# Attention with its order written out per pair of steps, a table of PSUM banks, two more turned heads, and turned rows kept by quarters

## The chip, the cores and the metric

The kernel runs on one core of a Trainium2 chip. A core has five engines, each with its own queue of instructions that it takes in order: TensorE (PE in the profile; PEld is its loading of weights), VectorE (DVE), ScalarE (ACT), GpSimd (POOL) and SyncE (SP, which here only issues transfers). TensorE writes its products into banks of PSUM, from where VectorE and ScalarE read them. Transfers between DRAM and the core's memory run on 16 DMA engines. The metric is the device time of one execution in microseconds; the number given is the median of the runs.

## What is computed

A token mixer of two parallel branches on the same normalised rows: attention with 16 query heads that share one key head and one value head, and a two-layer network with GELU.

```python
S, D, H, Dh, F = 2048, 448, 16, 28, 1792
xn = layernorm(x)
# attention, on layernorm's output
q = (xn @ wq).reshape(S, H, Dh)
k, v = xn @ wk, xn @ wv
p = softmax(einsum("hqd,kd->hqk", q, k) * Dh ** -0.5)
a = einsum("hqk,kd->hqd", p, v) @ wo
# network, with a second normalisation
y = layernorm(xn)
m = gelu(y @ w1 + b1) @ w2 + b2
out = x + a + m
```

All of it is in float32; the kernel keeps most operands as a high and a low part to reach that precision.

## The kernel before

The kernel has three stages. The first loads x, normalises it, turns it and projects it to q, k and v; the projections are also written to DRAM. The second is the network. The third is attention, which runs as 16 units: a unit is one chunk of 512 queries with one group of four heads. A unit has 16 key tiles of 128 keys, taken two at a time, so that attention has 128 steps; two steps in a row are a pair of steps, 64 in all.

**Ordinary heads.** The softmax needs the largest score of each row ahead of time. For each head a stream of 16 products with the queries on the partitions (`max_stream`, L598) is reduced by VectorE (L599). The negated maximum of a unit goes into two extra rows of its queries (`load_max`). In attention each key tile and head then has one product with the keys on the partitions (L1032), and ScalarE takes its exponential into a buffer `p` (L1033). When all four heads of a key tile are there, `pv` multiplies the values with them in four matmuls side by side (L996), summed over the 16 tiles in one bank `po`.

**Turned heads.** For one head of each unit, and two heads of unit 15 (`TURNED`), the product is made once, with the queries on the partitions (`turned_scores`, L632). VectorE copies it into a buffer `raw` and takes its maximum in the same instruction (L633); ScalarE takes the exponential in two halves of 1024 columns (`turned_exp`, L650); four stores write the tile to DRAM (`td`, L653). Later `load_quarters` brings a quarter of the keys back with one transfer for each half of it (L840), and VectorE turns 32 x 32 blocks into the layout that L996 reads (`turn_blocks`, L1008). A turned head thus has 16 products where an ordinary one has 32.

Both streams begin in the second stage, where they fill gaps between the network's matmuls: 390 of the 752 maxima and 192 of the 272 turned products are made before attention. There are two `raw` buffers, so tile t + 2 waits until tile t is stored.

**What sets the order.** Attention's program is written by a loop that reads a string of letters for each pair of steps: s is a score with its exponential, m a maximum, t a turned product, x half an exponential of a turned tile, T a turn, n and o steps of the normalisation and of the output product, e `load_max`, a bar the second step's start, and a figure that many weighted sums. There are six such strings, one for most units' first pairs, one for their others, and four for the start and the end. Letters with nothing to do are passed over; m is held back by a share of the total (`WEIGHTS`, `LEAD`), and a figure takes only tiles of steps that are complete.

**PSUM banks.** Seven banks take scores, maxima, turned products and output products in attention (`m0` to `m6`), and one holds `po`. `mtile` takes the bank that a small plan with fixed prices of each operation believes free first.

Of the kernel before, what the change touches and what calls it, by code (L numbers as in the profile page):

```python
# [10 lines left out]
F32 = mybir.dt.float32  # L11
# [6 lines left out]
P = 128  # L18
S, D, H, DH, F = 2048, 448, 16, 28, 1792
NT = S // P  # L20
CT = 4
# [13 lines left out]
LEAD = 11  # L35
KEPT = 1, 2, 3
MLP_ORDER = 1, 2, 3, 0
NH = 8
# [4 lines left out]
def block_kernel(ctx, tc, x, wq, wk, wv, wo, w1, b1, w2, b2, out):  # L43
# [10 lines left out]
    free_at, clock = {}, dict(pe=0, a=0, d=0)  # L54
# [37 lines left out]
    wqp = ph1a.enter_context(tc.tile_pool(name="wqp", bufs=1))  # L92
    xin, first_raws = [], []
    for c in range(2):
        first_raw = keep.tile([P, 4, NT, 32], F32, name="raw", bufs=RAWS)
        first_raw = first_raw.rearrange("p r b i -> p (r b i)")[:, 0:CT * D].rearrange("p (k d) -> p k d", k=CT)
# [17 lines left out]
        for t in range(t0, t0 + n):  # L114
            nc.sync.dma_start(xin[t], xv[:, t, :])

    def mtile(shape, by="d"):
        if free_at:
            i = min(free_at, key=lambda i: free_at[i])
            clock["pe"] = max(clock["pe"], free_at[i]) + PRODUCT  # L120
            clock[by] = max(clock[by], clock["pe"] + LANDS) + READS[by]
            free_at[i] = clock[by] + LANDS
        else:
            i = banks["d"].popleft()
            banks["d"].append(i)
        return (mp if i < 3 else mp4).tile(shape, F32, name=f"m{i}")

    def rawtile(shape):
# [496 lines left out]

    def turned_scores(i):
        for t in range(CT):
            raw = keep.tile([P, 4, NT, 32], F32, name="raw", bufs=RAWS)
            m3 = keep.tile([P, 8], F32, name="m3", bufs=RAWS)
            for n in range(4):  # L630
                sc = mtile([P, CW])
                pe.matmul(sc, q3[i % 2][:, t * P:(t + 1) * P], ks[:, n * CW:(n + 1) * CW], start=True, stop=True)  # L632
                dve.tensor_scalar(raw[:, :, 4 * n:4 * n + 4, :].rearrange("p r b i -> p b r i"),  # L633
                                  sc.rearrange("p (b r i) -> p b r i", r=4, i=32), SCALE, -3e38,
                                  op0=ALU.mult, op1=ALU.max, accum_out=m3[:, n:n + 1])
# [9 lines left out]
    def turned_exp():  # L645
        if not exps:
            return
        u, t, raw, m3, h = exps.pop(0)
        rs = slice(2 * h, 2 * h + 2)
        act.activation(raw[:, rs], raw[:, rs], AF.Exp, bias=m3[:, 4:5], scale=1.0)  # L650
        if h == 1:
            for a in (0, 2, 1, 3):
                nc.sync.dma_start(td[u].rearrange("(r p) a k -> p a r k", p=32)[:, 4 * t + a],  # L653
                                  raw[32 * a:32 * a + 32].rearrange("p r b i -> p r (b i)"))
            stored[u] = t

    tq = Stream()
# [107 lines left out]
    for n in range(len(mslots) + 2):  # L765
# [22 lines left out]
        if c == NCH - 1 and 6 <= ft < 12:  # L788
            for i in (2 * ft - 12, 2 * ft - 11):
                q, r = divmod(i, 4)  # L790
                nc.sync.dma_start(ahead[q][:, 4 * r:4 * r + 4, :], td[0, 3][:, 4 * r:4 * r + 4, P * q:P * q + P])
        ts, pace = 0, 21
        if n == 2:
            pace = 20
# [25 lines left out]
    free_at.update((i, k) for k, i in enumerate((0, 1, 6, 3, 2, 4, 5)))  # L820

    def weights_tile():
        t = xl_p.tile([P, 4, CW], F32R, name="xl").rearrange("p b n -> p (b n)")
# [17 lines left out]

    pool.memset(wor, 0.0)
    woh = wol = None
# [12 lines left out]
    rows, worked = {}, []  # L856

    def load_rows_of(c, tiles):
        for k in tiles:
# [4 lines left out]
    def o_jobs(c, gs, tiles=range(CT)):  # L864
        last = NG - 1 in gs
        for k in tiles:
            po = mtile([P, D])
            ts = slice(k * P, (k + 1) * P)
            for g in gs:
                oth, otl = ots[c, g]  # L870
                pe.matmul(po, oth[:, ts], woh[:, g, :], start=(g == gs[0]), stop=False)  # L871
                pe.matmul(po, oth[:, ts], wol[:, g, :], start=False, stop=False)  # L872
                pe.matmul(po, otl[:, ts], woh[:, g, :], start=False, stop=(g == gs[-1]))  # L873
            a = rows[c, k]
            dve.tensor_add(a, a, po)
            if last:
                nc.sync.dma_start(ov[:, CT * c + k, :], a)
            worked.append(1)
            yield

    def o_tiles(c, g):
# [141 lines left out]
    def score(u, kt, j):  # L1023
        if not halfway:
            p = pair_of()
            halfway.append((p[:, 1], (id(p), 1)))
            p, key = p[:, 0], (id(p), 0)
        else:
            p, key = halfway.pop()
        taken[key] = u, kt  # L1030
        s = mtile([P, CW], "a")
        pe.matmul(s, ks[:, kt * P:(kt + 1) * P], qss[u][:, j, :], start=True, stop=True)  # L1032
        act.activation(p, s, AF.Exp, scale=SCALE)  # L1033
        ps[u, kt, j] = p
# [13 lines left out]
    left = total - maxed  # L1048
    weight = [0 if n >= len(steps) - LEAD else WEIGHTS[n % 2] for n, (u, kt) in enumerate(steps)]

    def begin(n):
        nonlocal loads
        u, kt = steps[n]
        if n == 0:
            loads = pool
        if n == len(steps) - 6:
            free_at.pop(6)
# [11 lines left out]
    for n0 in range(0, len(steps), 2):  # L1069
# [9 lines left out]
        kind = 0 if n0 == 0 else 5 if n0 >= len(steps) - 2 else 4 if u == NU - 1 else 3 if n0 > len(steps) - LEAD else 1 + (kt0 > 0)  # L1079
        for what in ORDERS[kind]:  # L1080
            if what == "|":
                n, kt = n0 + 1, kt0 + 2
                begin(n)
            elif what == "s":
                score(*jobs.pop(0))
            elif what == "m":
                if maxed < total - left + left * sum(weight[:n + 1]) / sum(weight):
                    maxed += mxs.step()
            elif what == "t":
                if tq.step():  # L1090
                    clock["d"] += 125
            elif what == "x":
                if exps:
                    clock["a"] = max(clock["a"], clock["pe"]) + 1041
                turned_exp()
            elif what == "T":
                if turn:
                    clock["d"] = max(clock["d"], clock["pe"]) + 1165
                    turn_blocks(u, *turn.pop(0))
            elif what == "e":  # L1100
                if kt >= 6 and u + 1 in mrs:
# [1 line left out]
            elif what == "n":  # L1103
                side.step()
            elif what == "o":
                if n >= len(steps) - 5 and not lasts:
                    lasts.append(oside.add(o_jobs(NCH - 1, range(NG - 1))))
                worked.clear()
                oside.step()
                if worked:  # L1110
                    clock["pe"] += 2200
                    clock["d"] += 2000
            elif what.isdigit():
                clock["pe"] += 320
                for _ in range(int(what)):
                    if pvq[0] in steps[:n] or (pvq[0][0], pvq[0][1] - 1) in steps[:n]:
                        pv(*pvq.pop(0))
                        clock["pe"] += 858
# [31 lines left out]
```

## Time and profile before

| | us |
|---|---|
| median of 3 runs (1064.3 to 1064.78) | 1064.61 |
| the profiled execution | 1064.65 |
| its span, first to last instruction | 1062.8 |
| TensorE busy | 1054.0 (99%) |
| VectorE busy | 903.6 (85%) |
| ScalarE busy | 723.5 (68%) |
| GpSimd busy | 563.2 (53%) |
| first score product of attention begins at | 480.8 |

The profile is of one execution. An engine's busy time is the time covered by records of its instructions; on TensorE records of neighbouring matmuls overlap, since the next one begins while the one before is still running out. A group of instructions has its line, engine and operation, what it writes and reads, its count, its busy time and the mean of one record in ns, and the idle time just ahead of its instructions with what ended it. A row of a stage gives its start and end, its length, then the busy time of each engine with the number of instructions, the granted share of TensorE's clock, the mean share of the DMA engines that was busy, and GB/s. A row of the timeline has the start, the length, the engine and the instruction, where instructions of one kind that follow each other are one row.

### The profile page before, as it was taken

The numbers are of one execution on the slowest core, as the hardware profiler recorded it, in microseconds if no ns is written. First come the engines' busy times: TensorE is split into PE (matmuls) and PEld (weight loads), VectorE is DVE, ScalarE is ACT, GpSimd is POOL, SyncE is SP. The second block draws the span as 40 slices with busy tenths as digits, with TensorE's granted clock in tenths as the row PEclk, the third lists the DMA queues.
The fourth block names the chain that finished last, engine by engine and source line by source line (L and its number), as shares of the span: only waits on it lengthen the run. The fifth ranks groups of instructions, "written<-read, shape, count | busy, mean of one in ns | idle before, by whom it ended". The sixth has DMA issues, their size and how long they took to land.

```text
span 1062.8 us, 17825 instructions
## 1 busy us (share of the span) xinstructions
PE 1054.0 (99%) x5805; PEld 711.2 (67%) x5805; DVE 903.6 (85%) x1890; ACT 723.5 (68%) x1240; POOL 563.2 (53%) x704
## 2 busy tenths in 40 slices
PE   9999999999999999999999999999999999999998
PEld 8778888888888888885555455655545644556455
DVE  7889999999999899998888888688887777776765
ACT  6775555655656655646888888588887687775773
POOL 6678787668766778874354434324333334343130
PEclk9999999999999999999999999999999999999999
DMA  9864455566665666955877888778788676775692
GB/s 269 250 225 151 121 152 163 151 187 182 196 182 167 180 205 195 286 165 151 225 230 217 227 235 234 193 222 225 212 235 233 187 215 177 182 182 144 181 286 77
DMA packets 222160, 209.86 MB, mean 197 GB/s; under 512 B 17854, under 2 KB 173668, under 8 KB 222068
## 3 DMA queue, kind: packets, MB, share of 16 engines
q1 hardware_dynamic: 209524, 187.28, 61.5%
q0 software_dynamic: 11136, 20.87, 8.0%
q8 instruction: 46, 0.75, 0.3%
q10 hardware_dynamic: 1408, 0.57, 0.2%
q14 instruction: 46, 0.38, 0.1%
HBM read 121.31 MB, written 86.10 MB: 195 GB/s over the span
## 4 chain that ended last, share of the span: by engine, by line
PE 96%; DVE 3%; ACT 1%; DMA 0%; issue 0%; ACTq 0%; DVEq 0%
PE po L996 20%; PE m L1032 18%; PE m L598 16%; PE m L715 12%; PE ph L192 11%; PE m L632 6%; PE qp L192 3%; DVE mx L599 1%; PE ph L195 1%; PE ph L197 1%; PE m L871 1%; PE m L873 1%; PE m L872 1%; PE po L979 1%; PE m L979 1%; PE qp L316 0%
## 5 line engine op out<-in xcount | busy, mean ns | idle before, releaser
L599 DVE TENSOR_REDUCE mx<-m 128x1 f32<-128x512 f32 x752 | 484.4, 682 | 89.5 <-PE m L598 87.6
L1033 ACT ACTIVATE p<-m 128x512 f32<-128x512 f32 x652 | 342.1, 622 | 102.7 <-PE m L1032 99.8
L598 PE MATMUL m<-ks,qm 128*128 128x512 f32 x752 | 288.5, 399 | 1.0 <-DVE mx L599 0.6
L1032 PE MATMUL m<-xh,ks 128*128 128x512 f32 x752 | 259.6, 413 | 0.5 <-DVE a L720 0.5
L996 PE MATMUL po<-p,vs 128*32 128x512 f32 x1664 | 219.5, 595 | 0.9 <-DVE p L1008 0.9
L1032 PEld LDWEIGHTS m<-xh,ks 128*128 128x128 f32 x752 | 137.6, 187 | 96.5 <-issue 40.0
L633 DVE TENSOR_SCALAR_CACHE_REDUCE raw<-m 128x512 f32<-128x512 f32 x272 | 181.7, 686 | 9.0 <-PE m L632 6.1
L598 PEld LDWEIGHTS m<-ks,qm 128*128 128x128 f32 x752 | 141.3, 188 | 40.8 <-issue 11.7
L650 ACT ACTIVATE raw<-raw,m 128x1024 f32<-128x1024 f32 x136 | 152.9, 1161 | 0.0
L1008 DVE STREAM_TRANSPOSE p<-quarter 128x1024 f32<-128x1024 f32 x114 | 139.9, 1233 | 1.8 <-DMA quarter<-td 1.5
L680 ACT ACTIVATE hx<-ph,b1t 128x512 f32<-128x512 f32 x55 | 37.9, 688 | 150.5 <-PE ph L197 99.0
L996 PEld LDWEIGHTS po<-p,vs 128*32 128x32 f32 x1664 | 55.0, 109 | 108.7 <-issue 105.2
L632 PE MATMUL m<-ks,q 128*128 128x512 f32 x272 | 107.1, 395 | 0.0
L696 POOL TENSOR_TENSOR hl<-hx,hh 128x512 fp32r<-128x512 f32 x56 | 72.7, 1299 | 32.5 <-ACT hh L694 32.4
L563 POOL DMA_DIRECT2D xh<-qd x60 | 37.7, 630 | 86.6 <-PE m L1032 76.7
L715 PE MATMUL m<-w2h,hl 128*128 128x448 f32 x224 | 81.3, 367 | 0.0
L715 PE MATMUL m<-w2h,hh 128*128 128x448 f32 x224 | 81.3, 366 | 0.0
L715 PE MATMUL m<-w2l,hh 128*128 128x448 f32 x224 | 81.2, 366 | 0.0
L684 POOL TENSOR_TENSOR hz<-hz,hx 128x512 f32<-128x512 f32 x56 | 72.8, 1300 | 4.6
L689 POOL TENSOR_TENSOR hx<-hx,hz 128x512 f32<-128x512 f32 x56 | 72.6, 1297 | 4.7
L1033 ACT ACTIVATE xh<-m 128x512 f32<-128x512 f32 x100 | 55.8, 623 | 21.8 <-PE m L1032 21.3
L682 POOL TENSOR_SCALAR hz<-hz 128x512 f32<-128x512 f32 x56 | 35.0, 624 | 56.6 <-ACT hz L681 56.5
(198 smaller groups left out, 1548.8 us busy)
## 6 DMA issues: line engine op xcount, KB each, us to landing
td<-raw SPq DMA_DIRECT2D x272, 256.0 KB
quarter<-td SPq DMA_DIRECT2D x130, 512.0 KB
xh<-qd POOLq DMA_DIRECT2D x56, 168.0 KB, 5.2
qd<-qe SPq DMA_DIRECT2D x24, 256.0 KB
a<-in_A_x_dram SPq DMA_DIRECT2D x24, 224.0 KB
qm<-qd SPq DMA_DIRECT2D x96, 56.0 KB
qm<-qd POOLq DMA_DIRECT2D x92, 56.0 KB, 4.2
ad<-a SPq DMA_DIRECT2D x16, 224.0 KB
```

What stands on the lines that cost most here:

```text
L192: pe.matmul(ps, w, v, start=(n == 0), stop=False)
L598: pe.matmul(pm, qm[:, t * P:(t + 1) * P], ks[:, n * CW:(n + 1) * CW], start=True, stop=True)
L599: dve.tensor_reduce(mx[:, CT * j + t, n:n + 1], pm, axis=AX.X, op=ALU.max)
L632: pe.matmul(sc, q3[i % 2][:, t * P:(t + 1) * P], ks[:, n * CW:(n + 1) * CW], start=True, stop=True)
L633: dve.tensor_scalar(raw[:, :, 4 * n:4 * n + 4, :].rearrange("p r b i -> p b r i"), sc.rearrange("p (b r i) -> p b r i", r=4, i=32), SCALE, ...
L650: act.activation(raw[:, rs], raw[:, rs], AF.Exp, bias=m3[:, 4:5], scale=1.0)
L684: pool.tensor_mul(hz, hz, hx)
L715: pe.matmul(m2[k], h[:, k * P:(k + 1) * P], w[:, ft, :], start=(ft == 0 and i == 0), stop=(ft == NF - 1 and i == 2))
L996: pe.matmul(po[32 * j:32 * j + 32, :], vs[:, kt, :], ps.pop((u, kt, j)), start=(kt == 0), stop=(kt == NT - 1))
L1008: dve.transpose(p.rearrange("p k (g j) -> p g k j", j=32), part[:, :, 32 * k:32 * k + 64].rearrange("p g (k j) -> p g k j", j=32))
L1032: pe.matmul(s, ks[:, kt * P:(kt + 1) * P], qss[u][:, j, :], start=True, stop=True)
L1033: act.activation(p, s, AF.Exp, scale=SCALE)
```

## The change

Three things change together.

1. The six strings become 64, one for each pair of steps, and the plan behind `mtile` becomes a table of 1193 figures, the bank of each tile of attention in turn. The gates on m are gone. A figure may take a key tile as soon as its four heads have been issued, and many strings hold two or three figures.
2. `TURNED` gains the second head of units 11 and 13: 19 turned heads instead of 17.
3. The turned rows lie in DRAM by quarters of the keys. A tile's buffer `raw` is ordered the same way, each product filling one quarter. A store has 32 x 16 runs of 128 elements where it had 32 x 4 of 512; a load of half a quarter has 128 runs of 1024 elements where it had 128 x 8 of 128.

`turned_scores` also passes a step by while more than two halves await their exponential.

```diff
-WEIGHTS = 3, 5
-ORDERS = ("nsmsmsmsonsmsmst|sxnmsmsetssnmTmT2", "nxmnnsso|snsT4mtnsemnmsssmmsosstmsT", "snmTsmsmxnsmn4|smensmmssntsmssotsoT", "sTsnesnx4s|nssssossstsnoT", "TsTTnen4sT|nsssssosno", "nTss4sTonTss|nosTsns2")
-PRODUCT, LANDS, READS = 229, 200, {"a": 480, "d": 602}
-TURNED = tuple((u, 3) for u in range(16)) + ((15, 2),)
+ORDERS = (
+    "|sssmsmssmtmssmmmTssTtss",
+    "sm|ssss3smsttsmsstTssT",
...
+    "Tsss2msnsnstsmmm|sTssssmxxn3",
...
+)
+BANKS = (
+    "0163240513642015346203412503125064312560314526045231604521306451230465123460531246053214062153046123"
...
+)
+TURNED = tuple((u, j) for u in range(16) for j in ((3, 2) if u in (11, 13, 15) else (3,)))
...
-    td = {h: dram.tile([P, 4 * CT, 512], F32, name=f"td{h[0]}_{h[1]}") for h in TURNED}
+    td = {h: dram.tile([4, P, 4 * CT, P], F32, name=f"td{h[0]}_{h[1]}") for h in TURNED}
...
-    def mtile(shape, by="d"):
-        if free_at:
-            i = min(free_at, key=lambda i: free_at[i])
-            clock["pe"] = max(clock["pe"], free_at[i]) + PRODUCT
-            clock[by] = max(clock[by], clock["pe"] + LANDS) + READS[by]
-            free_at[i] = clock[by] + LANDS
-        else:
-            i = banks["d"].popleft()
-            banks["d"].append(i)
+    def mtile(shape):
+        i = int(places.pop(0)) if places else banks["d"][0]
+        banks["d"].append(banks["d"].popleft())
...
-            raw = keep.tile([P, 4, NT, 32], F32, name="raw", bufs=RAWS)
+            while len(exps) > 2:
+                yield
+            raw = keep.tile([P, 4, 4, P], F32, name="raw", bufs=RAWS)
...
-                dve.tensor_scalar(raw[:, :, 4 * n:4 * n + 4, :].rearrange("p r b i -> p b r i"),
+                dve.tensor_scalar(raw[:, n].rearrange("p r (b i) -> p b r i", i=32),
...
-                nc.sync.dma_start(td[u].rearrange("(r p) a k -> p a r k", p=32)[:, 4 * t + a],
-                                  raw[32 * a:32 * a + 32].rearrange("p r b i -> p r (b i)"))
+                nc.sync.dma_start(td[u].rearrange("q (r p) a k -> p a (q r) k", p=32)[:, 4 * t + a],
+                                  raw[32 * a:32 * a + 32].rearrange("p q r k -> p (q r) k"))
...
-            nc.sync.dma_start(part, td[u, j][:, at, P * q:P * q + P])
+            nc.sync.dma_start(part, td[u, j][q, :, at])
...
-        for what in ORDERS[kind]:
+        for what in ORDERS[n0 // 2]:
...
-                if maxed < total - left + left * sum(weight[:n + 1]) / sum(weight):
-                    maxed += mxs.step()
+                maxed += mxs.step()
...
-                    if pvq[0] in steps[:n] or (pvq[0][0], pvq[0][1] - 1) in steps[:n]:
+                    if all((*pvq[0], j) in ps for j in range(4)):
                         pv(*pvq.pop(0))
```

Lines of the changed kernel have other numbers; the instructions that the text speaks of stand there at L668 and L669 (maxima, before L598 and L599), L704 and L705 (turned products, L632 and L633), L1068 (weighted sums, L996), L1080 (turns, L1008), L1104 (scores, L1032), L912 (a mark that a quarter's buffer is free, L839), L725 (stores, L653) and L913 (loads of quarters, L840).

The order of TensorE in the second pair of steps of unit 6, before: scores (`m<-xh,ks`), maxima (`m<-ks,qm`) and one block of sums (`po<-p,vs`, four matmuls for each sum).

```order
L598 MATMUL m_8106<-ks,qm_160 128x512
L1032 MATMUL m_8109<-xh,ks 128x512
L1032 MATMUL m_8117<-xh,ks 128x512
L996 MATMUL po<-p,vs 32x512 x16
L1032 MATMUL m_8140<-xh,ks 128x512
L598 MATMUL m_8143<-ks,qm_160 128x512
L578 MATMUL m_8146<-ident,mr 12x128
L1032 MATMUL m_8155<-xh,ks 128x512
```

The same place now, from the first of its two blocks of sums; the second, of 12 matmuls, stands after 15 products.

```order
L1104 MATMUL m_8107<-xh,ks 128x512
L1068 MATMUL po<-p,vs 32x512 x8
L668 MATMUL m_8119<-ks,qm_163 128x512
L1104 MATMUL m_8122<-xh,ks 128x512
L1104 MATMUL m_8126<-xh,ks 128x512
L1104 MATMUL m_8129<-xh,ks 128x512
L704 MATMUL m_8134<-ks,q_165 128x512
L1104 MATMUL m_8137<-xh,ks 128x512
```

One block of four sums became blocks of two and of three, with products between them; over attention 61 blocks of whole sums become 73.

The order of VectorE in unit 13, before: turns (`p<-quarter`), maxima, and marks of a free quarter.

```order
L1008 STREAM_TRANSPOSE p<-quarter 128x16x2x32
L839 MEMSET quarter 1x1
L599 TENSOR_REDUCE mx<-m_10912 128x1
L1008 STREAM_TRANSPOSE p<-quarter 128x16x2x32
L599 TENSOR_REDUCE mx<-m_10919 128x1
L599 TENSOR_REDUCE mx<-m_10925 128x1
```

And now, in the same unit, where two heads are turned:

```order
L1080 STREAM_TRANSPOSE xh<-quarter 128x16x2x32
L1080 STREAM_TRANSPOSE p<-quarter 128x16x2x32
L912 MEMSET quarter 1x1
L669 TENSOR_REDUCE mx<-m_10947 128x1
L912 MEMSET quarter 1x1
L654 SCALAR_TENSOR_TENSOR mn<-m_10955,mn 12x128
L948 TENSOR_TENSOR a<-a,m_10962 128x448
L1080 STREAM_TRANSPOSE p<-quarter 128x16x2x32 x2
```

Unit 13 has 16 turns where it had 8, in twos at some places. Before the first score of attention, the order of instructions on every engine is the old one but for the shape of the stores and of the first quarters' loads.

More of the change, by code (lines that the diff above doesn't have):

```diff
@@ L28 @@
 PAIRS = 13
-WEIGHTS = 3, 5
-ORDERS = ("nsmsmsmsonsmsmst|sxnmsmsetssnmTmT2", "nxmnnsso|snsT4mtnsemnmsssmmsosstmsT", "snmTsmsmxnsmn4|smensmmssntsmssotsoT", "sTsnesnx4s|nssssossstsnoT", "TsTTnen4sT|nsssssosno", "nTss4sTonTss|nosTsns2")
-PRODUCT, LANDS, READS = 229, 200, {"a": 480, "d": 602}
-TURNED = tuple((u, 3) for u in range(16)) + ((15, 2),)
+ORDERS = (
+    "|sssmsmssmtmssmmmTssTtss",
+    "sm|ssss3smsttsmsstTssT",
+    "smmss|sm3essmtsTxmsssstsT",
+    "T|x4mmsstTssmsssssm2smss",
+    "mmsssmTxxsstmTmss4smn|sntsss",
+    "smm2nmsmsmmsststst|Tntxsmss3enmTsmnxs",
+    "ssssm3TsmnsmssttmsTsss|n",
+    "ssxnmsTtsnxn22msnsmmmssssnsTs|",
+    "ssstT2smsst|msmssssTs",
+    "ssT|2msntmsTstsxmmnsmmx4smsnnstmsts",
+    "|ssmTnmnnTsses3smssstssmsmxmm",
+    "sns3sssTsmm|smnnstmmtm2snssmmsntT",
+    "sssTssxnssm4mnsnmmsss|mtsT",
+    "sss|2mmsmssxtmnnTsmssnxs3snsT",
+    "|tmsmsssstsnssTTe21tmssssx",
+    "sT|smsss1nn4Tmmxsntnssmmsmsss",
+    "sssTmsnnms3Tmsmsmtnsssms|sto",
+    "ntsT4xxsnsnTms|stmnstsmmssmnsnsns",
+    "o2nooTmsmosmosesnsmttmTsm3msmssmsmsno|mnxos",
+    "smTssTmx|4stsmnstsmsstsss",
+    "Ts|mmssT3tsmmmsmsmxmtsossmsnmsnmtsmm",
+    "sns|sTsssnx6nmssmsmTmtsossm",
+    "smsnssmssmmstosmst|sexxTTnss",
+    "ssTmsn213|snsmsmtnsnsTosmmssntns",
+    "sstTsmxstxsts31mstssmTtnss|s",
+    "Tsss2msnsnstsmmm|sTssssmxxn3",
+    "tennmTTstnsssnmssnss4sms|sms",
+    "mssmsssn|tssmTmsTsn3nttssmms",
+    "ssxxmmTnsmssst1T3mntsm|ssnsss",
+    "Ttsnsxtn21s|mnsssxTsmmses2msmss",
+    "ssmtssmsnsstnT|s4xTmsmssms",
+    "nssnstsxmTsm2mTsssssnsmtt|2s",
+    "Tssnmnmtsnstsxxtmmss3on|mmosstnnsTsms",
+    "smT|osso4smesnsmsmmmsssnmsnTs",
+    "smnst2x2T|tsmsnsmssmosmxmosTssns",
+    "msn3|sTmsmnsmossmnsnttsmsstxsTxmos",
+    "sTs5mstsmsstsTmmmsso|tssttmsx",
+    "sTtsoxssststnmnms2xsmmssxnsmnT|s",
+    "ssmsnns5smnesTstmssm|osmssT",
+    "sstsnss|Tmsnn3smtssmmnTsss",
+    "ms|stnxsTm4Tsmssnssssss",
+    "mm|xT2mtnmssnsm11mnnstssmsstsssTs",
+    "sTm2|esnnsmssmtssmnnxmsmxsntT3msstmms",
+    "so|tTstssmmTmm1n3smnssmsssnmmnsms",
+    "|sTsTm5nTmnmnsmsnntssTss",
+    "Ts|ssTTTss5msesnmsm",
+    "ssssxssT111s|TTTs",
+    "snmsssss|nTxsTT5Tntsn",
+    "smmsmsssmsnttsssnnTm|mxsm3mmmnosTs",
+    "Tmsmms|smsn4nmtxesnmstsnTsssmomsts",
+    "nmn3|osmsmsmsmosmnmsossTmTssomsmsn",
+    "4on1TnnmssmnTtsssssm|1smsmssms",
+    "sTm3oTmmssnTnsmnm|omssssT",
+    "msmxnsnomTssTtt4nstnmm|TssnTs",
+    "ssm|sneonTnTssmsmm4TmssT",
+    "mTmsmnsns5xmsTTTs|mmsss",
+    "stsT4mmxnsss|snnossnmssTss",
+    "sxnssmm31ssmTsssssm2Tmsnm|s",
+    "ssmsmTs1enssnssss|snTs",
+    "ss4ssssssTsnns|2Tss",
+    "TnssssssTssT1n|11T",
+    "nnTsss|ssTTsT3ss",
+    "ssssssTn5n|sToTTs",
+    "sTssosTs|sossoT212T",
+)
@@ L94, in block_kernel @@
     for c in range(2):
-        first_raw = keep.tile([P, 4, NT, 32], F32, name="raw", bufs=RAWS)
-        first_raw = first_raw.rearrange("p r b i -> p (r b i)")[:, 0:CT * D].rearrange("p (k d) -> p k d", k=CT)
+        first_raw = keep.tile([P, 4, 4, P], F32, name="raw", bufs=RAWS)
+        first_raw = first_raw.rearrange("p q r k -> p (q r k)")[:, 0:CT * D].rearrange("p (k d) -> p k d", k=CT)
         first_raws.append(first_raw)
@@ L819, in block_kernel @@
     op = ctx.enter_context(tc.tile_pool(name="op", bufs=1, space=PSUM))
-    free_at.update((i, k) for k, i in enumerate((0, 1, 6, 3, 2, 4, 5)))
+    places.extend(BANKS)
+    banks["d"] = collections.deque((0, 1, 2, 3, 4, 5))
     def weights_tile():
@@ L854, in prep_wo @@
         pool.tensor_sub(wol[:, g, :], wor[:, g, :], f(woh[:, g, :]))
-    rows, worked = {}, []
+    rows = {}
     def load_rows_of(c, tiles):
@@ L1047, in block_kernel @@
     total = 4 * CT * len(heads)
-    left = total - maxed
-    weight = [0 if n >= len(steps) - LEAD else WEIGHTS[n % 2] for n, (u, kt) in enumerate(steps)]
     def begin(n):
```

34 lines of the change are left out of this document (15 added, 19 removed).

## The prediction

> **What bounds the kernel now.** I read the first two parts of the page, then the busy time by stage, then the groups of the last stage, then the timeline of TensorE alone. The page:
>
> ```profile
> span 1062.8 us, 17825 instructions
> PE 1054.0 (99%) x5805; PEld 711.2 (67%) x5805; DVE 903.6 (85%) x1890; ACT 723.5 (68%) x1240; POOL 563.2 (53%) x704
> PEclk9999999999999999999999999999999999999999
> PE 96%; DVE 3%; ACT 1%; DMA 0%; issue 0%; ACTq 0%; DVEq 0%
> ```
>
> TensorE is never long idle, its clock is granted in full, and it holds 96% of the chain that ended last. But matmul records overlap, so 99% busy does not say that nothing is lost. By stage (us; TensorE, weight loads, VectorE, ScalarE and GpSimd busy; clock, DMA share, GB/s):
>
> ```profile
> 60.00:430.00 370.00, 368.95 (x1673) 310.57 (x1672) 353.28 (x772) 218.13 (x304) 279.32 (x273) 1.00 0.60 175
> 480.80:1058.70 577.90, 576.49 (x3577) 309.04 (x3575) 454.77 (x896) 437.97 (x827) 204.09 (x323) 1.00 0.75 204
> ```
>
> The second row is attention, from the first score (L1032) to the last matmul: 577.9 us, and all of the reordering is there. Its groups:
>
> ```profile
> L599 DVE TENSOR_REDUCE mx<-m 128x1 f32<-128x512 f32 x362 | 233.5, 676 | 86.2 <-PE m L598 86.2
> L1032 PE MATMUL m<-xh,ks 128*128 128x512 f32 x752 | 259.6, 413 | 0.5 <-DVE a L720 0.5
> L996 PE MATMUL po<-p,vs 128*32 128x512 f32 x1664 | 219.5, 595 | 0.9 <-DVE p L1008 0.9
> L598 PE MATMUL m<-ks,qm 128*128 128x512 f32 x362 | 134.6, 404 | 0.0
> L996 PE MATMUL po<-xh,vs 128*32 128x512 f32 x256 | 64.7, 595 | 0.0
> L632 PE MATMUL m<-ks,q 128*128 128x512 f32 x80 | 31.8, 398 | 0.0
> ```
>
> What one costs is the distance between starts, not the mean of a record. The timeline of TensorE:
>
> ```profile
> 639.22 0.65 PE L1032 MATMUL m<-xh,ks 128*128 128x512 f32 x2
> 639.80 2.35 PE L996 MATMUL po<-p,vs 128*32 128x512 f32 x19
> 641.56 0.59 PE L996 MATMUL po<-xh,vs 128*32 128x512 f32 x1
> ...
> 641.99 0.59 PE L996 MATMUL po<-xh,vs 128*32 128x512 f32 x1
> ...
> 643.37 0.50 PE L1032 MATMUL m<-xh,ks 128*128 128x512 f32 x1
> 643.71 0.39 PE L598 MATMUL m<-ks,qm 128*128 128x512 f32 x1
> 643.94 0.39 PE L1032 MATMUL m<-xh,ks 128*128 128x512 f32 x1
> 644.17 0.62 PE L598 MATMUL m<-ks,qm 128*128 128x512 f32 x2
> ```
>
> From 643.71 to 643.94 and to 644.17, a product of 512 columns takes 0.23 us (0.228 over longer pieces). A weighted sum (four heads, one key tile) is two passes of four matmuls, 0.43 apart (641.56, 641.99): 0.86 us. A block of four sums should take 3.44 and takes 3.57 (639.80 to 643.37); the product ahead of it lasts 0.12 longer than 0.23 and the first one behind it 0.11 longer (0.34). So each change from products to sums and back costs about **0.35 us**, whatever the block's size.
>
> Attention adds up so: 752 + 362 + 80 = 1194 products at 0.228 = 272.2; 240 sums in whole (1920 records by 8) and 16 in halves, 256 at 0.86 = 220.2; 180 output matmuls at 0.20 = 36.0; 65 blocks of sums at 0.35 = 22.8. That is 551.2 of 577.9. Of the other 26.7, some 4 lie behind the last sum and 3 in the small transposes ahead of new maxima. About **20 us** are waits of a product for its PSUM bank, as the waits of the weight loads show (total, times, longest):
>
> ```profile
> PEld m L1032 <- ACT p L1033: 29.9, 136, 0.3
> PEld m L598 <- ACT p L1033: 6.8, 26, 0.3
> ```
>
> Many waits, none over 0.3 us, partly hidden behind the running matmul. VectorE and ScalarE are not full, but they must be fed while TensorE is in its sums, and seven banks are all the stock they have.
>
> **The change part by part.** *Two more turned heads.* Each gives up 16 maximum products and 16 score products for 16 turned ones. The order has 720, 330 and 112 products in attention: 32 fewer, 32 x 0.228 = **-7.3 us** of TensorE. VectorE loses 32 maxima and gains 32 turned reads, 8 small reductions and 16 turns. Its prices, by distance of starts:
>
> ```profile
> 604.16 1.24 DVE L1008 STREAM_TRANSPOSE p<-quarter 128x1024 f32<-128x1024 f32 x1
> 605.33 0.69 DVE L599 TENSOR_REDUCE mx<-m 128x1 f32<-128x512 f32 x1
> ...
> 609.25 1.89 DVE L599 TENSOR_REDUCE mx<-m 128x1 f32<-128x512 f32 x3 [0.67 <-PE m L598]
> 611.06 0.68 DVE L633 TENSOR_SCALAR_CACHE_REDUCE raw<-m 128x512 f32<-128x512 f32 x1
> ```
>
> A turn takes 1.17, a maximum (611.06 - 609.25) / 3 = 0.60, and I take 0.61 for a turned read. So +32 x 0.01 + 8 x 0.08 + 16 x 1.17 = +20 us: from 362 x 0.60 + 80 x 0.61 + 136 x 1.17 + some 20 of small work = 445 to 465 us. That lies beside TensorE while its stage lasts longer. ScalarE gives up 32 exponentials and gains 16 of double width, which is about even. The 32 further stores and 16 further loads go to SP's queue, which does nothing but transfers; I cost them at nothing beside 545 us of TensorE work, until a turn waits for its quarter. On GpSimd the two heads' columns are loaded into the turned heads' buffers instead of the maxima's, 8 loads either way, and its other steps move with the order. What TensorE could wait for there is the next head's columns:
>
> ```profile
> qm<-qd POOLq DMA_DIRECT2D x92, 56.0 KB, 4.2
> ```
>
> They land in 4.2 us. Between their issue and their first use the order has at least 9.5 us of TensorE work before and 11.3 now, so I cost this at nothing too; 16 times some 2 us if GpSimd were held up.
>
> *The order.* The blocks of sums become 76 (73 in whole, 3 in halves), 11 more: 11 x 0.35 = **+3.9 us**. In return the run of products between blocks falls from about 20 to about 16, so fewer products stand behind seven banks. No row shows the new waits. From below they are bounded by nothing (-20 us). From above, two units of this profile, 0 and 1:
>
> ```profile
> 480.80:515.20 34.40, 32.99 (x182) 17.06 (x180) 29.17 (x57) 25.66 (x50) 9.12 (x15) 1.00 0.65 185
> 515.20:550.50 35.30, 35.30 (x211) 17.92 (x211) 30.15 (x63) 31.01 (x60) 18.75 (x27) 1.00 0.78 218
> ```
>
> Unit 1 has 81 products (18.5), 16 sums (13.8) and 4 blocks (1.4): 33.7, so it loses 1.6. Unit 0 has 82, 12 and 3, 30.1, and loses 4.3: its sums start late, and TensorE runs ahead of its readers. So a unit loses 1.6 where the feeding goes well and 4.3 where it does not. Counted in the two orders, products that take a bank last used five or six products before, with no sum between, fall from 196 to 136. By that count 20 us become 14; with shorter blocks, over which the readers' stock lasts better, I take **12**, nearer to the count than to nothing: **-8 us**.
>
> *The bank table* costs no time of its own: it names the bank that the planner chose before, and its worth is in those waits.
>
> *Turned rows by quarters.* A store of 256 KB becomes 512 packets of 512 bytes instead of 128 of 2 KB, a load of 512 KB 128 packets of 4 KB instead of 1024 of 512 bytes; per head 9216 packets instead of 10240. The trace has a stage with many 2 KB stores (60 to 430: 175 GB/s at a share of 0.60, 292 at a full share) and one where 512-byte loads rule (204 at 0.75, 272 at a full share). The four stores of a tile, 1 MB, take 3.6 us of all engines by the first and 3.9 by the second. Is there room? The stage before attention, SP's and VectorE's rows:
>
> ```profile
> 218.51 10.01 SPq L653 DMA_DIRECT2D td<-raw  x8
> 222.46 4.62 DVE L599 TENSOR_REDUCE mx<-m 128x1 f32<-128x512 f32 x7
> 227.38 0.69 DVE L633 TENSOR_SCALAR_CACHE_REDUCE raw<-m 128x512 f32<-128x512 f32 x1 [0.30 <-PE m L632]
> ```
>
> The stores start at 218.51, and the same buffer is written again at 227.38: 8.9 us for 3.9, and VectorE waited there for TensorE, not for a transfer. I cost it at nothing, bounded by 46 tiles before attention at 0.3 either way, 14 us if that cover were gone. Order and counts before attention stay as they are, so its 480.8 us stay.
>
> [...]
>
> **The sum.** The profiled execution took 1064.65 us, 1062.8 of span and 1.85 around it; the runs shown have a median of 1064.61, the same. 1064.65 - 7.3 + 3.9 - 8 = **1053 us**.
>
> **The rivals.**
>
> *All bank waits go.* For it: no wait is over 0.3 us, and both readers have idle time in sum (VectorE 445 of 578). Against: 136 tight reuses remain. It gives 1064.65 - 7.3 + 3.9 - 20 = 1041 us.
>
> *The order moves the waits only.* Eleven more blocks are paid for, and the waits of 20 us stay. For it: bank and reader prices are the same. It gives 1064.65 - 7.3 + 3.9 = 1061 us; with 3 us more of waits it is no change.
>
> *VectorE becomes the limit (slower).* By the order, units 12 and 13 together have 56 maxima, 9 turned reads and 24 turns: 33.6 + 5.5 + 28.1 and some 3.5 of small work = 70.7 us of VectorE. TensorE has 145 products (33.1), 31 sums (26.7), 36 output matmuls (7.2), 9 blocks (3.2): 70.2. No slack is left there, and units 2, 4 and 8 (36 maxima and turned reads each) are near: 21.7 + 9.4 + 0.8 = 31.9 beside some 34 of TensorE. If in each of these five units the loss is unit 0's 4.3 instead of 1.6, and the waits elsewhere stay, 1061 + 13.5 = 1075 us. It decides from 4 us of such losses on, where 1065 is reached. Against it: over all of attention VectorE has 465 of some 565 us, and its reads are spread over the unit.
>
> *The stores are slower than the loads show (slower).* If a 512-byte packet into DRAM took over twice its share, 1 MB would need over the 8.9 us there are, and VectorE would stand still at each of 46 tiles; 1 us each is +46, some 1099 us.
>
> *The change does not do what it says.* The order shows 32 products fewer and 76 blocks, so only the timing is open.
>
> **How the numbers follow.** Chances: the forecast, 1047 to 1059, 0.60; nearly all waits gone, 1041 to 1047, 0.10; waits moved, 1059 to 1067, 0.18; VectorE the limit 0.09; stores 0.03. The range of 1044 to 1067 leaves out half of the second and the last two cases, 0.17. A measurement of this kernel can tell about 0.2% (2.1 us) from no change. Faster by more than that (under 1062.5) are the first two and 0.10 of the third: 0.80; within it 0.08; slower 0.12.
>
> **What would show it.** Attention should end some 12 us earlier with 480.8 us before it unchanged. In its groups L1032 has 720, L598 330 and L632 112. The waits of weight loads for L1033 should fall in sum. Right for the stores: VectorE's turned reads still wait for TensorE and for no DMA. Wrong: waits of TensorE's products for VectorE's maxima or turns in units 12 and 13 (the VectorE rival), sums that wait for a turn, or a longer stage before attention (the stores).

## The result and the profile after

The changed kernel takes **1056.0 us** (median of 4 runs, 1053.39 to 1056.62) where the kernel before takes 1064.65 (1064.3 to 1064.78): a ratio of 0.9915, with a 95% interval of 0.9897 to 0.9932. That is faster by 8.6 us, where 11.6 were forecast; 1056.0 lies in the range. The runs spread over 3.2 us where those of before spread over 0.5.

The page of the changed kernel, profiled in the run of 1055.69 us: span, engines, and the chain that ended last by engine.

```profile
span 1052.8 us, 17905 instructions
PE 1043.8 (99%) x5773; PEld 708.9 (67%) x5773; DVE 926.9 (88%) x1962; ACT 720.6 (68%) x1224; POOL 563.1 (53%) x704
PE 94%; DVE 3%; DMA 1%; ACT 1%; SPq 0%; issue 0%; ACTq 0%; DVEq 0%
```

TensorE still bounds it, VectorE has 23 us more work, and transfers have come into the chain with 1%. The span is 10.0 us shorter, and 1.0 us more lies around it (2.9). By stage, with the columns of the prediction's rows (TensorE, weight loads, VectorE, ScalarE, GpSimd; clock, DMA share, GB/s):

```profile
60.00:430.00 370.00, 368.96 (x1673) 310.65 (x1672) 353.24 (x772) 218.17 (x304) 279.29 (x274) 1.00 0.66 174
480.75:1048.70 567.95, 565.70 (x3545) 306.16 (x3543) 478.03 (x968) 435.07 (x811) 203.97 (x323) 1.00 0.79 236
```

The stretch before attention holds the same work as before; the DMA engines are busier there for the same GB/s (0.66, before 0.60), which is the price of the smaller stores. Attention begins at the same 480.8 us and has lost the 10 us (567.95, before 577.9). Its groups, and the weight loads' waits (total, times, longest):

```profile
L1104 PE MATMUL m<-xh,ks 128*128 128x512 f32 x720 | 229.8, 405 | 2.1 <-DVE raw L705 1.1 <-DVE a L792 0.5 <-DVE mx L669 0.5
L669 DVE TENSOR_REDUCE mx<-m 128x1 f32<-128x512 f32 x330 | 212.8, 679 | 51.3 <-PE m L668 50.5
L668 PE MATMUL m<-ks,qm 128*128 128x512 f32 x330 | 123.9, 409 | 0.1
L705 DVE TENSOR_SCALAR_CACHE_REDUCE raw<-m 128x512 f32<-128x512 f32 x112 | 75.1, 680 | 11.5 <-PE m L704 6.4 <-DMA td<-raw 4.9
```

```profile
PEld m L1104 <- ACT p L1105: 16.6, 48, 0.8
PEld m L668 <- ACT p L1105: 9.3, 22, 0.8
```

The waits of scores for a bank that ScalarE still reads (L1104, before L1032) have fallen from 136 to 48 and from 29.9 to 16.6 us; those of maxima have grown a little, from 6.8 to 9.3. The longest of them has grown from 0.3 to 0.8 us. A weight load can wait while TensorE still works, so these sums, 25.9 us here, are not lost time; what TensorE loses is worked out from its starts further down, 11.8 us. The 32 products are gone. New is the last entry at L705: turned reads wait 4.9 us for a store of `raw`, which none did before. The timeline shows the longest of them, SP's, VectorE's and TensorE's rows:

```profile
507.86 3.33 SPq L725 DMA_DIRECT2D td<-raw  x4
...
514.35 1.24 DVE L1080 STREAM_TRANSPOSE p<-quarter 128x1024 f32<-128x1024 f32 x1
519.17 0.69 DVE L705 TENSOR_SCALAR_CACHE_REDUCE raw<-m 128x512 f32<-128x512 f32 x1 [3.59 <-DMA td<-raw]
...
516.92 1.90 PE L1068 MATMUL po<-p,vs 128*32 128x512 f32 x16
519.92 0.50 PE L1104 MATMUL m<-xh,ks 128*128 128x512 f32 x1 [1.10 <-DVE raw L705]
```

The four stores of a tile are issued from 507.86 on, and its buffer is free at 519.17, 11.3 us later. VectorE stands still for 3.59 us, and then TensorE for 1.10 and, at 522, once more for 0.51, since VectorE reads no bank in that time.

### The profile page after: what moved, and what is told of

It is laid out like the page before. It is cut to its first block, busy times and chain, and to the rows that moved or that the text cites. A ratio compares the mean times of both kernels' runs of the same rounds, so it can differ in the third digit from the quotient of the medians.

```text
span 1052.8 us, 17905 instructions
## 1 busy us (share of the span) xinstructions
PE 1043.8 (99%) x5773; PEld 708.9 (67%) x5773; DVE 926.9 (88%) x1962; ACT 720.6 (68%) x1224; POOL 563.1 (53%) x704
## 4 chain that ended last, share of the span: by engine, by line
PE 94%; DVE 3%; DMA 1%; ACT 1%; SPq 0%; issue 0%; ACTq 0%; DVEq 0%
PE po L1068 20%; PE m L1104 16%; PE m L668 16%; PE m L787 12%; PE ph L262 11%; PE m L704 7%; PE qp L262 3%; DVE mx L669 1%; PE ph L265 1%; PE ph L267 1%; PE m L944 1%; PE m L946 1%; PE m L945 1%; DMA td<-raw 1%; PE po L1051 1%; PE m L1051 1%
## 5 line engine op out<-in xcount | busy, mean ns | idle before, releaser
L669 DVE TENSOR_REDUCE mx<-m 128x1 f32<-128x512 f32 x720 | 463.6, 683 | 54.6 <-PE m L668 51.9
L1105 ACT ACTIVATE p<-m 128x512 f32<-128x512 f32 x622 | 323.6, 623 | 90.1 <-PE m L1104 88.8
L668 PE MATMUL m<-ks,qm 128*128 128x512 f32 x720 | 277.7, 401 | 1.1 <-DVE mx L669 0.6
L1104 PE MATMUL m<-xh,ks 128*128 128x512 f32 x720 | 229.8, 405 | 2.1 <-DVE raw L705 1.1
L1068 PE MATMUL po<-p,vs 128*32 128x512 f32 x1664 | 221.8, 596 | 0.0
L705 DVE TENSOR_SCALAR_CACHE_REDUCE raw<-m 128x512 f32<-128x512 f32 x304 | 202.4, 686 | 20.0 <-PE m L704 12.5
L1104 PEld LDWEIGHTS m<-xh,ks 128*128 128x128 f32 x720 | 131.6, 188 | 69.2 <-ACT p L1105 16.6
L722 ACT ACTIVATE raw<-raw,m 128x1024 f32<-128x1024 f32 x152 | 170.3, 1158 | 3.2 <-DVE m L711 3.1
L668 PEld LDWEIGHTS m<-ks,qm 128*128 128x128 f32 x720 | 134.2, 188 | 55.9 <-issue 12.6
L1080 DVE STREAM_TRANSPOSE p<-quarter 128x1024 f32<-128x1024 f32 x128 | 155.5, 1229 | 4.9 <-PE m L1104 3.1
L1068 PEld LDWEIGHTS po<-p,vs 128*32 128x32 f32 x1664 | 54.7, 109 | 105.0 <-issue 101.4
L704 PE MATMUL m<-ks,q 128*128 128x512 f32 x304 | 119.0, 398 | 0.0
L704 PEld LDWEIGHTS m<-ks,q 128*128 128x128 f32 x304 | 57.0, 188 | 20.2 <-issue 2.5
L1068 PE MATMUL po<-xh,vs 128*32 128x512 f32 x256 | 68.7, 596 | 0.0
L633 POOL DMA_DIRECT2D xh<-qd x60 | 38.0, 634 | 56.7 <-PE m L1104 34.4
```

Source lines behind the costliest of these rows:

```text
L668: pe.matmul(pm, qm[:, t * P:(t + 1) * P], ks[:, n * CW:(n + 1) * CW], start=True, stop=True)
L669: dve.tensor_reduce(mx[:, CT * j + t, n:n + 1], pm, axis=AX.X, op=ALU.max)
L705: dve.tensor_scalar(raw[:, n].rearrange("p r (b i) -> p b r i", i=32), sc.rearrange("p (b r i) -> p b r i", r=4, i=32), SCALE, -3e38, op0= ...
L1068: pe.matmul(po[32 * j:32 * j + 32, :], vs[:, kt, :], ps.pop((u, kt, j)), start=(kt == 0), stop=(kt == NT - 1))
L1080: dve.transpose(p.rearrange("p k (g j) -> p g k j", j=32), part[:, :, 32 * k:32 * k + 64].rearrange("p g (k j) -> p g k j", j=32))
```

## The experiments

The theory: 32 products are worth 7.3 us, blocks cost 3.9, bank waits fall by about 8, and the one wait for a store takes back some 3. Rivals: the heads are worth nothing because VectorE pays for them; the order did it without the table; the quarters cost throughout. All of these kernels do the whole computation, in other orders or layouts. "Rows as before" means 2 KB stores and 512-byte loads.

**The rows as before, in the new order (e1_old_rows).** The changed kernel with these lines of before:

```diff
-    td = {h: dram.tile([4, P, 4 * CT, P], F32, name=f"td{h[0]}_{h[1]}") for h in TURNED}
+    td = {h: dram.tile([P, 4 * CT, 512], F32, name=f"td{h[0]}_{h[1]}") for h in TURNED}
...
-                dve.tensor_scalar(raw[:, n].rearrange("p r (b i) -> p b r i", i=32),
+                dve.tensor_scalar(raw[:, :, 4 * n:4 * n + 4, :].rearrange("p r b i -> p b r i"),
...
```

> The changed kernel with the turned rows laid out in DRAM and in the raw buffer as before (2 KB stores, 512-byte loads). Theory: the order alone makes VectorE's wait for a store at 519 us (3.6 us), since the reuse of that raw buffer stands closer to its store than any before; the layout costs nothing. Then 1056 us within 1.5, and the wait for td<-raw stays at 3 to 4 us. Rival (the 512-byte stores land late): the wait goes and the time falls to 1052 to 1053 us. Rival (the larger loads are worth something): 1058 us or more.

1052.99 us (1052.0 to 1053.6), 3.0 less than the changed kernel: the rival on late stores, though the wait does not go altogether. Its timeline, SP's and VectorE's rows at the same place:

```profile
507.41 3.49 SPq L725 DMA_DIRECT2D td<-raw  x4
...
514.30 1.23 DVE L1080 STREAM_TRANSPOSE p<-quarter 128x1024 f32<-128x1024 f32 x1
516.73 0.69 DVE L705 TENSOR_SCALAR_CACHE_REDUCE raw<-m 128x512 f32<-128x512 f32 x1 [1.20 <-DMA td<-raw]
```

The tile is stored in 9.3 us instead of 11.3, VectorE waits 1.20 instead of 3.59, and the wait now falls inside TensorE's block of sums. So both have a part: the order put the reuse so close that 9.3 us are not quite enough, and the smaller stores made them 11.3. The DMA engines are full at that time in both kernels, and with the smaller stores they move less. The row of 510 to 515 us, first of the changed kernel, then of this one:

```profile
510.00:515.00 5.00, 5.00 (x29) 3.23 (x21) 3.78 (x8) 4.58 (x10) 1.29 (x2) 1.00 1.08 283
```

```profile
510.00:515.00 5.00, 5.00 (x29) 3.22 (x21) 3.77 (x7) 4.58 (x10) 1.29 (x2) 1.00 1.05 327
```

TensorE has the same instructions in the same order in both traces, so that their starts can be laid side by side. The spans differ by 2.8 us; the changed kernel falls behind by 2.2 of them between 518 and 522.3 us, around this one wait, and nowhere else by more than 0.15 at a time.

**The rows by quarters, in the old order (e3_rows_alone).** The kernel before with only the third edit of the change.

> The kernel before with only the rows laid out by quarters. Theory: no difference, 1064.6 us within 0.6, and no wait of VectorE for a store, since stores of 1 MB take 3.9 us of 8.9. Rival (512-byte stores land late): waits of turned reads for td<-raw and 1067 us or more. Rival (4 KB loads relieve the DMA engines): 1062 us or less.

1064.48 us, ratio 0.9999 (0.999 to 1.0009): no difference. Its stages:

```profile
60.00:430.00 370.00, 368.99 (x1672) 310.50 (x1671) 353.18 (x772) 217.96 (x303) 279.38 (x273) 1.00 0.66 174
480.80:1058.70 577.90, 576.50 (x3576) 309.18 (x3575) 454.82 (x896) 437.95 (x827) 204.26 (x323) 1.00 0.69 204
```

The share of the DMA engines rises from 0.60 to 0.66 where stores rule, a tenth more engine time, and falls from 0.75 to 0.69 where loads do, at the same GB/s; with the old order's distance between a store and the next use of its buffer (in attention 10.7 us at the least, from the first store's issue) neither is felt.

**One product moved (e7_t_moved).** The changed kernel, one letter of one string:

```diff
-    "mmsssmTxxsstmTmss4smn|sntsss",
+    "mmsssmTxxssmTmss4tsmn|sntsss",
```

> The changed kernel with one turned product, the first of unit 1's first pair of steps, moved behind the block of four sums, about 4 us later; rows by quarters. Theory: the one wait of VectorE for a store at 519 us is what the quarters cost: it goes, and the time falls by 2.5 to 3 us to 1053 us within 1. Rival (the quarters cost elsewhere too, or the product is missed where it goes): 1055 us or more.

1052.42 us (1051.75 to 1052.94). Of VectorE's waits for stores this is left:

```profile
DVE raw L705 <- DMA td<-raw: 0.9, 2, 0.6
```

One letter gives the 3 us back with the rows by quarters kept. What the quarters cost is this one meeting. (The table names banks tile by tile, so the tiles that the product passed now take others; by this run and the next that cost nothing.)

**Both (e8_old_rows_t_moved).** The two edits above together.

> The new order with 19 turned heads, the rows as before (e1_old_rows, 1053.0 us) and the turned product of e7_t_moved behind its block. Theory: of the wait for a store, 1.2 us were left with 2 KB stores and TensorE lost nothing by them there: the same as e1_old_rows and e7_t_moved, 1052.5 us within 1. Rival (what both took away adds up): 1050.5 us or less.

1052.48 us (1052.07 to 1053.16). They do not add up, as two remedies of one wait should not. e7, e1 and e8 cannot be told apart. Their twelve runs (1051.75 to 1053.6) lie below three of the changed kernel's four, and far below the kernel before.

**The heads alone (e2_heads_alone).** The kernel before with the new `TURNED`, and in units 11 and 13 its two strings with four scores taken out of each and two turns put in:

```diff
-TURNED = tuple((u, 3) for u in range(16)) + ((15, 2),)
+TURNED = tuple((u, j) for u in range(16) for j in ((3, 2) if u in (11, 13, 15) else (3,)))
...
+        if u in (11, 13):
+            kind = 6 + (kt0 > 0)
         for what in ORDERS[kind]:
```

> The kernel before with the second heads of units 11 and 13 turned; in these two units four scores of each pair of steps give way to two more turns, everything else of its order, its planner and its rows stays. 32 products fewer, 61 blocks of sums as before. Theory: 32 x 0.228 = 7.3 us less, waits as before: 1057 us, 1056 to 1059. Rival (VectorE is the limit where the heads are turned, the order had to make room for them): 1062 us or more, with units 11 and 13 longer by what VectorE gains.

1081.27 us (1079.13 to 1082.26): slower by 16.7, as the rival has it and far above its 1062 us. Units 11, 12 and 13 of this kernel, in the columns of the stages; they take 125.2 us, in the kernel before 108.7:

```profile
878.80:915.50 36.70, 34.73 (x193) 15.69 (x193) 36.55 (x69) 23.60 (x41) 15.13 (x26) 1.00 1.08 281
915.50:956.60 41.10, 37.57 (x208) 17.67 (x207) 29.82 (x70) 27.98 (x52) 10.73 (x18) 0.92 0.84 232
956.60:1004.00 47.40, 43.09 (x241) 23.69 (x241) 40.93 (x78) 23.79 (x41) 13.63 (x22) 1.00 1.00 274
```

VectorE's busy time in unit 11 (the third after the length) is 36.55 of 36.70 us. The old order keeps giving this unit maxima and turned reads at its even pace on top of twice the turns, and VectorE is the bound there. In units 12 and 13 it is not full; what adds to the loss is that TensorE, around stops of 3.53 and 1.69 us, ran at half its clock for 6.83 us in unit 12 and 3.41 in unit 14 (last section). By an estimate, half of that time, this is 5 of the 16.7 us. The changed kernel's units 11 to 13:

```profile
880.10:907.00 26.90, 26.90 (x188) 11.54 (x188) 25.55 (x42) 19.52 (x38) 6.91 (x12) 1.00 0.88 277
907.00:943.50 36.50, 36.50 (x218) 19.27 (x218) 34.60 (x75) 26.36 (x51) 15.95 (x25) 1.00 0.89 258
943.50:978.40 34.90, 34.90 (x216) 20.58 (x215) 32.86 (x59) 19.16 (x37) 13.49 (x21) 1.00 0.82 264
```

VectorE has 25.55 of 26.90 there, and 93 of the 98.3 us of the three units: nearly full, but TensorE is never seen idle (26.90 of 26.90 and so on). The strings give unit 11 only 8 maxima and 2 turned reads and put the others elsewhere.

**The order with 17 heads (e6_order_alone).** The new strings and table with the rows as before; the last 32 letters t became m, and in units 11 and 13 half of the turns became two scores each, in the bank used longest ago.

```diff
...
-    "|sTsTm5nTmnmnsmsnntssTss",
+    "|sTsSSm5nTmnmnsmsnnmssSSss",
...
```

> The new order and table with 17 turned heads and the rows as before: the last 32 turned products of the strings become maxima, units 11 and 13 get four scores and lose two turns in each pair of steps (the added scores take the bank used longest ago). 32 products more than e1_old_rows (1053.0 us). Theory: the heads are worth their 7.3 us of products in this order: 1060 us, 1058 to 1062. Rival (VectorE's 20 us more eat it): 1053 us or less.

1078.87 us, far from both. Units 0 to 10 last as long as those of e1 to 0.3 us each, but unit 11 lasts 37.2 us (27.0 in e1) and unit 13 50.5 (34.8), where 16 products each explain 3.6. The scores put in by hand are new to the order, and so are the banks that they take; which of the two costs so much, the run cannot tell. It does not price the heads. The next two do, taken together.

**The planner in place of the table (e5_planner_banks).** e1 with `mtile` and its prices as before.

> The new order with 19 turned heads and the rows as before (e1_old_rows, 1053.0 us), with the planner of the kernel before choosing the banks in place of the table. Theory: the table is part of what lowered the bank waits; its loss gives back about half of the 7 to 9 us that they fell: 1057 us, between 1055 and 1061. Rival (the order alone did it, any sensible choice of bank will do): 1053 us within 1.

1066.6 us (1066.42 to 1068.4): 13.6 more than e1, over three times what was expected, with TensorE's instructions in the same order. The weight loads' waits, first of this kernel (L1112 are its scores, L676 its maxima), then of e1:

```profile
PEld m L1112 <- ACT p L1113: 29.8, 99, 0.9
PEld m L676 <- ACT p L1113: 16.6, 50, 0.8
```

```profile
PEld m L1104 <- ACT p L1105: 16.6, 48, 0.8
PEld m L668 <- ACT p L1105: 10.0, 22, 0.8
```

Twice as many products meet a bank that ScalarE still reads. The new order with the planner's banks is no faster than the kernel before, which took 1064.84 us beside it.

**The same with 17 heads (e10_planner_17_heads).** e5 with `TURNED` as before, the surplus t made m, and plain strings for units 11 and 13, such as

```diff
-    "ssssxssT111s|TTTs",
+    "sms4mseTmssnss|smnnsTsmessxnm",
```

> Like e5_planner_banks (new order, banks by the planner of before, rows as before, 19 heads, 1066.6 us) with 17 turned heads: the last turned products of the strings become maxima, and units 11 and 13 have plain strings with 12 scores, 2 turns and one or two blocks for each pair of steps. 32 products more, 73 + 3 blocks as there. Theory: the heads are worth their 7.3 us of products: 1074 us, 1071 to 1077. Rival (what VectorE gains by two heads costs as much): 1067 us or less.

1074.17 us (1073.78 to 1074.54), 7.6 more than e5, or 8.0 if each is taken from the kernel before that ran beside it. The strings of units 11 and 13 are rewritten, so work moves between units as well: unit 11 is 8.4 us longer than in e5, unit 14 5.2 shorter. In sum TensorE has as many blocks of sums in both, 32 products more here, and waits between products that differ by 1.3 us (table below). With one way of choosing banks, and an order that has room for them, the two heads are worth about their 32 products.

**Banks in turn (e11_banks_in_turn).** e1 with the seven banks taken in turn:

```diff
-        i = int(places.pop(0)) if places else banks["d"][0]
-        banks["d"].append(banks["d"].popleft())
+        i = banks["d"].popleft()
+        banks["d"].append(i)
...
```

> The new order of e1_old_rows (1053.0 us) with its seven banks taken in turn instead of by the table or the planner. Theory: the table was worth 13.6 us against the planner since a product that takes a bank too early stops TensorE; banks in turn know nothing of a reader's delay either: 1066 us or more. Rival (it was the planner that chose badly, for prices that do not fit this order): 1058 us or less.

1077.91 us (1076.18 to 1078.81), 24.9 more than e1 with TensorE's instructions in the same order. So the planner was not a bad choice; the table is a much better one for this order. Two stretches of 3.41 us at half clock (the mean clock of this profile is 0.997) are in these 24.9.

**Blocks split (e4_blocks_split).** The kernel before with 4 in the two common strings split in two:

```diff
...
-"nxmnnsso|snsT4mtnsemnmsssmmsosstmsT", "snmTsmsmxnsmn4|smensmmssntsmssotsoT"
+"nxmnnsso|snsT2mtnsemnms2ssmmsosstmsT", "snmTsm2smxnsmn|smensmmss2ntsmssotsoT"
...
```

> The kernel before with each block of four sums in the strings of ordinary pairs split into two blocks of two, one in each step: 119 blocks instead of 61. Theory: 58 x 0.35 = +20 us for the blocks, less what shorter runs save of the 20 us of waits; if they save half of it, 1075 us, between 1065 and 1085. Rival (a block costs nothing in itself, its price was only the wait of the first products): 1064 us or less. Rival (the waits do not depend on the blocks' size): 1085 us.

1137.04 us, 72 more, which no theory had. The waits of its weight loads:

```profile
PEld po L996 <- DVE quarter L839: 37.7, 53, 1.1
PEld po L996 <- ACT p L1033: 18.5, 64, 0.4
```

Now the sums wait (`po`), 53 times for VectorE and 64 times for ScalarE: split this way, they come straight behind the turns and exponentials that they read. So this run does not price a block; the next one does.

**Blocks parted at their place (e9_blocks_parted).**

```diff
...
-"nxmnnsso|snsT4mtnsemnmsssmmsosstmsT", "snmTsmsmxnsmn4|smensmmssntsmssotsoT"
+"nxmnnsso|sn2sT2mtnsemnmsssmmsosstmsT", "snmTsmsmxn2s2mn|smensmmssntsmssotsoT"
...
```

> The kernel before with each block of four sums in ordinary pairs parted into two blocks of two with two scores (or one score) between, at the old place, so that no sum comes sooner behind its turn: 118 blocks instead of 61. Theory: 57 x 0.34 = 19 us more, and the waits stay about what they were, since the blocks stand close together: 1084 us, 1080 to 1089. Rival (TensorE's loss in e4_blocks_split was the blocks, not the sums that waited for turns): 1130 us or more. Rival (a block's price is only waits that move): 1070 us or less.

1081.77 us, 16.9 more for 57 blocks: 0.30 us each, near the 0.35 read from the timeline. The waits of its scores' weight loads have grown as well (29.9 us before):

```profile
PEld m L1032 <- ACT p L1033: 54.4, 143, 0.8
```

But the loads wait while sums still run. Away from the blocks, TensorE loses 17.3 us between products where it lost 18.9 (table below); at the blocks, the changes from product to sum and from sum to product take 15.7 us more, 0.28 for each of the 57. The price of a block is real, and parting blocks buys almost nothing of the waits, 1.6 us.

## Why the prediction was right, and where it was not

*The 32 products, -7.3.* Borne out: 7.6 to 8.0 between e10 and e5, with two units' strings rewritten.

*The blocks, +3.9.* 11 blocks at 0.30 are 3.3 us by e9.

*The bank waits, -8.* By e1, which has all but the quarters: 1052.99 - 1064.59 = -11.6, and with -7.6 for the heads and +3.3 for the blocks some 7.3 are left, against 8 forecast. The traces also give the term directly. Where a product of attention follows a product, the distance between their starts above 0.228 us is what TensorE lost there, for the most part to a bank; the first distance behind a block is left out, since it belongs to the block.

| | distances | us above 0.228 each |
|---|---|---|
| the kernel before | 1038 | 18.9 |
| the changed kernel | 994 | 11.8 |
| its order and table, rows as before (e1) | 994 | 10.5 |
| its order, the planner's banks (e5) | 994 | 24.7 |
| the same with 17 heads (e10) | 1026 | 26.0 |
| its order, banks in turn (e11) | 994 | 32.6 |
| the old order with blocks parted (e9) | 981 | 17.3 |

So the 20 us of waits were well read, and they fell by 8.4 in e1: the size of the term is right. Its reason is right only in part. The prediction put the term under the order, because shorter runs of products stand behind the seven banks, and gave the table no price of its own. But parting the blocks took only 1.6 us off the waits (e9), and the new order with the planner's banks has more of them than the old one, not fewer (e5, e10); with 17 heads it is slower than the kernel before by 9.8 us (e10). In these runs the waits fall only when the table is there, and it takes off 13.6 (e5 against e1). The count of tight reuses, which gave 6, is of the order and the banks that it takes, and was a fair sign of both together; the 2 us that the prediction added to it for shorter blocks have no run behind them. "It names the bank that the planner chose before" was no reason to expect nothing more of it.

*The quarters at nothing.* This is the step that failed, by 3.0 us (e1), and it is all of the 3 us between 1053 and 1056. That the smaller packets alone do not lengthen the kernel held in the old order (e3). The cover was read at the wrong place. 8.9 us for 3.9 were measured ahead of attention and in the old order, and the 3.9 us are the bytes' time with all engines to themselves, an estimate from 204 GB/s at a share of 0.75; among other transfers a tile took 9.3 us (e1) or 11.3. At 508 us of the new one, a tile's first store was issued 2.1 us after its exponential, behind loads of quarters and of `wo` in the same queue; the DMA engines were full (a share of 1.08 from 510 to 515); and VectorE was ready to use the buffer again 7.7 us after that first issue, where in attention's old order at least 10.7 pass. The distance alone does not decide: at 736 us of the changed kernel a buffer was written again 6.7 us after its first store, with 0.69 us of wait. The bound given, 0.3 us for each of 46 tiles before attention, priced another mechanism.

*VectorE the limit.* The rival did not decide in the changed kernel, though VectorE is nearly as full in units 12 and 13 as it said (67.5 us busy of 71.4; it had reckoned with 70.7 of 70.2). e2 shows that it was no idle fear: the heads alone in the old order make VectorE the bound in unit 11 and cost 16.7 us.

*What would show it.* Attention is 10 us shorter (12 were forecast), 480.8 stands, the counts are right, ScalarE's bank waits fell. The sign named for the stores, turned reads that wait for a DMA, appeared, in attention and not before it.

Open: why the runs spread over 3 us. With the wait for the store out of the way they still spread over 1.2 to 1.6 (e7, e1). Open too is what lies around the span: 2.1 to 3.2 us in the runs of the changed kernel, where the sum kept the 1.85 of before.

## What to carry to other kernels

An order, a table of buffers and a division of work that are fitted to each other are to be judged together: here the heads alone cost 16.7 us, the order with another choice of banks gains nothing, and all three gain 11.6 (e1). Where an edit is costed at nothing because other work covers it, the cover is to be measured in the order that will run, at each place where it is needed and with what else runs there, since the same change of order that pays elsewhere can take it away; here one letter of a string gave it back.

## What the runs showed of the hardware

In e2 a stop of TensorE cost more than its length. TensorE waits 3.53 us, for a ScalarE that had waited for the full VectorE, and then runs at half its clock: three products take 1.65 us there, and 0.86 at 911.68. The two rows of its timeline:

```profile
917.76 1.15 ACT L650 ACTIVATE raw<-raw,m 128x1024 f32<-128x1024 f32 x1 [2.63 <-DVE m L639]
919.45 1.65 PE L1032 MATMUL m<-xh,ks 128*128 128x512 f32 x3 [3.53 <-ACT xh L1033]
```

The half clock begins at 918.58, before the stop ends, and lasts 6.83 us. The same kernel has another such stretch, of 3.41 us, behind a stop of only 1.69 us at 1006. Rows of 3.41 us before and within the two (TensorE's busy time comes first behind the length, the clock is the third figure from the right):

```profile
915.17:918.58 3.41, 0.75 (x3) 0.37 (x2) 3.38 (x8) 0.82 (x1) 0.86 (x2) 1.00 0.98 293
918.58:921.99 3.41, 2.54 (x11) 1.14 (x15) 2.09 (x5) 2.39 (x5) 0.00 (x0) 0.50 0.95 289
1003.91:1007.32 3.41, 1.72 (x9) 0.73 (x12) 3.38 (x8) 2.56 (x4) 0.38 (x1) 1.00 0.30 86
1007.32:1010.73 3.41, 3.41 (x21) 0.84 (x24) 0.23 (x1) 0.65 (x2) 0.00 (x0) 0.50 1.07 291
```

In e11 a longer stop, 2.75 us up to 1000.87, leaves the clock alone; it lies across these two rows:

```profile
996.31:999.72 3.41, 1.81 (x8) 1.14 (x7) 3.41 (x4) 3.05 (x6) 1.76 (x3) 1.00 0.74 256
999.72:1003.13 3.41, 2.27 (x21) 0.83 (x25) 3.38 (x9) 0.60 (x1) 0.00 (x0) 1.00 0.66 208
```

So the length of one stop did not decide in these two runs; what does, no run shows. The changed kernel's longest stop in attention, 1.10 us, left the clock at 1.00.
